# A layer norm's inverse root, in the attention layers, on POOL in place of DVE

## The chip, the cores and the metric

One Trainium2 chip, one of its cores. The time is the device time of one execution of the whole program in microseconds; lower is better. The engines are named as in the profile: PE (TensorE) multiplies matrices, DVE (VectorE), ACT (ScalarE) and POOL (GpSimd) work element by element, SP (SyncE) issues the transfers. Each engine takes its instructions in the order in which they were built, and an instruction whose operands aren't ready holds up all that stand behind it on its engine.

## The reference

A residual stream `x` of 2048 tokens by 640 runs through four layers. Layers 1 and 3 mix by a Fourier transform, layers 2 and 4 are attention over a window of 256 tokens, with 32 heads of 20.

```python
x = x + A(_layernorm(x))      # Real(DFT_seq(DFT_hidden(x))), as products with matrices
x = x + B(_layernorm(x))      # attention
x = x + A(_layernorm(x))
x = x + B(_layernorm(x))

def _layernorm(x, axis=-1, eps=1e-5):
    m = jnp.mean(x, axis=axis, keepdims=True)
    v = jnp.var(x, axis=axis, keepdims=True)
    return (x - m) / jnp.sqrt(v + eps)

def B(x):                      # q, k, v from x @ wqkv, H = 32, Dh = 20, W = 256
    scores = einsum("bhqd,bhkd->bhqk", q, k) * Dh ** -0.5
    scores = where(0 <= idx[:, None] - idx[None, :] < W, scores, -1e9)
    return einsum("bhqk,bhkd->bhqd", softmax(scores), v) -> (B, S, D) @ wo
```

## The kernel before

The tokens stand in 16 tiles of 128, a token to a partition. All products are made of pairs of 16-bit parts (a high part and a low part of what is left), so every operand is split: ACT writes the high part, DVE or POOL the low one. `spectral` computes the Fourier layers, `attention` the others; both are called twice, and this text counts attention layers 0 and 1.

**The loop of an attention layer** runs over `g`, 256 steps (16 tiles by 16 pairs of heads) and 12 more that finish. In each step `scores(g)` lets PE write the scores of one tile and pair into the tile `sp`, of which there is one buffer; DVE masks them (L1054) and takes their maximum `m` (L1058). Every fourth step the maxima are split into `tops` (L1064, L1065), and PE's transposes of them (`hand_on`, `copy_tops`) put them into `qs`. Seven steps later `by_key` makes the scores again, keys first, into `tp`, ACT turns them into weights `ptq` (L1102), and every other step POOL cuts the window's edges out of them with two selects (L1107, L1109). Thirteen steps later PE multiplies four heads' weights with `v` into `pv` (`values`); `back` divides, and POOL makes the two parts `os` of the output (L1153, L1154). What else PE has to do is handed out between these by a list of units `fill` (`run_fill`, `turn_unit`): the projections of the next block of two tiles (results `qf`, then `early`), products with `wo` (`out_tile`; for the last block `last_out`, in pieces), transposes.

**The norms in this loop** are generators in a queue `slow`; `slow_step`, once a step, runs the first of them up to its next `yield`. `rows_norm` normalises the two tiles of the block after next, `next_norm` (in layer 0 alone) each output tile for the Fourier layer that follows. Both use `norm_steps` and then `split` the result `lny` into `xs`: ACT the high part (L165), POOL the low one (L166); PE transposes `xs` later (`rows_turn`, `next_turn`), ACT and DVE copy the result (`xto`, `early`). For one tile a norm is two steps of statistics (L129, L132), two of the root (L138 to L142: eight instructions of one column, an estimate by bits and three rounds of Newton, each reading what the one before wrote) and the last step `lny` (L154). For the two tiles of `rows_norm` the statistics of both come first, then both roots, then both last steps. In `spectral` the norms are called with `act`, so that ACT makes the last step and DVE one instruction more (L146); that form is not touched.

**What sets the order.** The code is traced in the order in which the loop calls it, and a scheduler places each engine's instructions from that order and their dependencies. What `slow_step` traces stands under `tc.issue_after(topped[0])`: instructions of DVE are kept behind the newest maximum or part of the tops. This holds on DVE alone; instructions that the same step traces on another engine are not tied to it. In an attention layer PE's products and SP's transfers keep the traced order (`in_turn`).

After step 256 of layer 0 the last two tiles' products are finished in `last_out`, their norms are run by `next_norm` in the loop's last steps and in the loop behind it, eight at a time, and the next Fourier layer's first splits (`cc` from `cq` and `cs`, by `take_c`, on POOL, ACT and DVE) and products (`Hidden.stage`) stand among them.

Of the kernel before, what the change touches and what calls it, by code (L numbers as in the profile page):

```python
# [15 lines left out]
OP = mybir.AluOpType  # L16
# [46 lines left out]
def body(ctx: ExitStack, tc: tile.TileContext, x_in, cmat, whid, wqkv, wo, out):  # L63
    nc = tc.nc
# [42 lines left out]
    normed = [None]  # L107
# [14 lines left out]
    def norm_steps(xs, ys, act=False):  # L122

        n = len(xs)
        mv = keep.tile([P, n, 2], F32, tag=f"lnmv{n}", name="lnmv", bufs=2)
        for k, x in enumerate(xs):
            st = keep.tile([P, 2, 6], F32, tag="lnst", name="lnst", bufs=2)
            for h in range(2):
                nc.vector.bn_stats(st[:, h], x[:, h * 320:(h + 1) * 320])  # L129
                if h == 0:  # L130
                    yield
            nc.vector.bn_aggr(mv[:, k], st.rearrange("p a b -> p (a b)"))  # L132
            yield
        t = keep.tile([P, 3, n], F32, tag=f"lnt{n}", name="lnt", bufs=2)
        ts = nc.vector.tensor_scalar
        for k in range(n):
            h, g, u = (t[:, m, k:k + 1] for m in range(3))
            ts(h, mv[:, k, 1:2], 1e-5, -0.5 * X_UP ** -2, op0=OP.add, op1=OP.mult)  # L138
            ts(g.bitcast(I32), h.bitcast(I32), -0.5, ROOT, op0=OP.mult, op1=OP.add)
            for m in range(3):  # L140
                ts(u, g, g, h, op0=OP.mult, op1=OP.mult)  # L141
                normed[0] = ts(g, u, 1.5, g, op0=OP.add, op1=OP.mult).ins  # L142
                if m == 0:
                    yield
            if act:
                normed[0] = ts(u, mv[:, k, 0:1], g, -1.0, op0=OP.mult, op1=OP.mult).ins  # L146
            yield
        for k, x in enumerate(xs):
            g, u = t[:, 1, k:k + 1], t[:, 2, k:k + 1]
            y = keep.tile([P, D], F32, tag="lny", name="lny", bufs=2)  # L150
            if act:
                nc.scalar.activation(y, x, AF.Identity, bias=u, scale=g)
            else:
                normed[0] = ts(y, x, mv[:, k, 0:1], g, op0=OP.subtract, op1=OP.mult).ins  # L154
            ys.append(y)
            yield

    def layer_norm(xs):
        ys = []
        for _ in norm_steps(xs, ys, True):  # L160
            pass
        return ys
# [181 lines left out]
    def spectral(layer, res_src, hidden, first):  # L344
        with ExitStack() as st:
# [95 lines left out]
            def side_norm(s):  # L441
                x, ys = load_x(s), []
                for _ in range(3):
                    yield 1
                for _ in norm_steps([x], ys, True):
                    yield 1
                split_x(s, ys[0], nc.gpsimd)
                yield 1
# [853 lines left out]
```

## Time and profile before

| what | value |
| --- | --- |
| runs, median of 3 (lowest to highest) | 2277.91 us (2277.79 to 2279.62) |
| the profiled execution | 2273.16 us |
| its span, first to last instruction | 2271.4 us |
| granted clock of PE | 0.987 |
| busy, of the span: PE, DVE, POOL, ACT | 94%, 72%, 61%, 57% |
| attention layer 0, attention layer 1 | about 595 to 1210 us, 1700 to 2271 us |

The profile is one execution. Busy is the time in which an engine had at least one instruction under way; a matmul's record holds its way through the pipeline too, so PE's 94% overstates how much of its peak is used. The chain of waits is followed back from the last instruction: at each step to the instruction that released it, or to the one before it on the same engine; it tells which work was late, not by how much. A group's row holds line, engine, operation, names and shapes, count, busy time, mean of one in ns, and the idle time ahead of it. A row of waits holds the total in us, how often, and the longest. The trace names tiles by their role: `x` stands for the residual tiles.

### The profile page before, as it was taken

The page shows a single profiled execution, that of the slowest core. Times are in us where ns is not written, and L with a number is a line of the kernel's source. Part 1 is how long each engine was busy: PE and PEld are TensorE (multiplying, and loading weights), DVE is VectorE, ACT ScalarE, POOL GpSimd, SP SyncE. Part 2 cuts the span into 40 slices and gives each one's busy share as a digit, 9 for nine tenths or more (in the row PEclk, how much of TensorE's full clock was granted, in tenths as well). Part 3 has the DMA queues.
Part 4 walks back from the last instruction along what each step waited for, and adds up shares of the span by engine and source line. Part 5 has one row for each costly group of instructions (what it writes and reads, how often), then busy time and mean ns, then how long its engine had stood idle before and what let it go on. Part 6 is the DMA issues. An engine that isn't in the chain of part 4 may idle for free.

```text
span 2271.4 us, 55086 instructions
## 1 busy us (share of the span) xinstructions
PE 2132.5 (94%) x21985; PEld 1498.7 (66%) x21985; DVE 1632.5 (72%) x3577; ACT 1291.8 (57%) x2159; POOL 1387.0 (61%) x1788
## 2 busy tenths in 40 slices
PE   7989889899899999999898999999998999999997
PEld 4757666667666666677555777777676666777664
DVE  7886758866678787886756858585757777777664
ACT  6434455443367777777754443433434777777775
POOL 5775868857355665565445858586674545566443
PEclk9999999999999999999999999999999999999999
DMA  7664646454532322333324536363643323332231
GB/s 247 214 214 136 211 162 213 162 194 165 138 83 68 94 75 72 92 90 86 129 76 142 195 130 207 112 207 137 254 125 97 81 57 83 93 95 56 56 76 36
DMA packets 187605, 292.94 MB, mean 129 GB/s; under 512 B 13908, under 2 KB 120660, under 8 KB 178004
## 3 DMA queue, kind: packets, MB, share of 16 engines
q1 hardware_dynamic: 187348, 289.43, 40.9%
q8 instruction: 172, 2.82, 0.5%
q14 instruction: 85, 0.70, 0.1%
HBM read 202.51 MB, written 86.87 MB: 127 GB/s over the span
## 4 chain that ended last, share of the span: by engine, by line
PE 61%; DVE 14%; issue 5%; POOL 4%; ACT 3%; DMA 2%; SPq 0%; DVEq 0%; POOLq 0%; ACTq 0%
PE pf L116 25%; PE pv L116 8%; PE y L116 8%; PE z L116 5%; PE x L116 5%; PE sp L116 5%; DVE m L1058 3%; DVE sp L1054 3%; PE tp L116 3%; PE pt L116 2%; DVE cc L488 2%; ACT ptq L1102 1%; DMA x<-x2d 1%; DVE lnt L141 1%; PE acc L116 1%
## 5 line engine op out<-in xcount | busy, mean ns | idle before, releaser
L116 PEld LDWEIGHTS <-cc 128*128 128x128 f16 x5376 | 526.7, 98 | 220.6 <-issue 17.6
L1102 ACT ACTIVATE ptq<-tp,shift,alpha 128x768 f32<-128x768 f32 (+2 forms) x512 | 486.7, 951 | 176.1 <-PE tp L116 166.0
L116 PEld LDWEIGHTS <-big 128*128 128x128 f16 x4320 | 410.6, 99 | 148.7 <-issue 34.0
L1058 DVE TENSOR_REDUCE m<-sp 128x2 f32<-128x512 f32 (+1 forms) x512 | 344.9, 674 | 16.7
L1054 DVE COPY_PREDICATED sp<-mask,sp 128x256 f32<-128x256 int32 x448 | 191.0, 426 | 203.0 <-PE sp L116 186.7
L1107 POOL TENSOR_SCALAR_AFFINE_SELECT ptq<-ptq 128x512 f32<-128x512 f32 x224 | 145.4, 649 | 261.2 <-ACT ptq L1102 260.5
L116 PE MATMUL pf<-early,big 128*128 128x256 f16 x2400 | 304.5, 273 | 0.0
L485 ACT ACTIVATE cc<-cs 128x512 f16<-128x512 f32 x256 | 151.6, 623 | 241.3 <-POOL cs L478 119.2
L116 PE MATMUL y<-zc,cc 128*128 128x320 f16 x1728 | 266.3, 301 | 6.4 <-DVE pf L511 6.1
L488 DVE SCALAR_TENSOR_TENSOR cc<-cs,cc 128x512 f16<-128x512 f32 x256 | 252.2, 1000 | 13.2 <-ACT cc L485 12.9
L116 PE MATMUL pf<-big 128*128 128x320 f16 x1680 | 243.7, 304 | 17.2 <-DVE zc L256 8.3
L488 DVE SCALAR_TENSOR_TENSOR cc<-cq,cc 128x512 f16<-128x512 f32 x192 | 192.2, 1002 | 0.1
L1109 POOL TENSOR_SCALAR_AFFINE_SELECT ptq<-ptq 128x512 f32<-128x512 f32 x256 | 164.1, 641 | 43.7 <-ACT ptq L1102 43.7
L116 PE MATMUL pv<-ptq,v 128*32 128x128 f32 (+1 forms) x3840 | 183.8, 331 | 0.0
L116 PE MATMUL z<-zc,cc 128*128 128x320 f16 x1152 | 179.7, 301 | 3.7 <-DVE res L511 3.7
L116 PE MATMUL x<-zc,cc 128*128 128x320 f16 x1152 | 180.2, 301 | 0.0
L116 PE MATMUL sp<-ks,qs 62*128 62x256 f16 (+1 forms) x1792 | 154.3, 249 | 17.2 <-DVE m L1058 15.1
L1079 ACT ACTIVATE qs<-pt 2x512 f16<-2x512 f16 x224 | 131.4, 586 | 47.8 <-PE pt L116 45.2
L116 PE MATMUL pf<-big,early 128*128 128x320 f16 x960 | 157.6, 300 | 0.8 <-DVE x L879 0.8
L116 PE MATMUL tp<-qs,ks 62*128 62x128 f16 x2688 | 150.6, 217 | 4.4 <-ACT ptq L1102 3.4
L116 PE MATMUL pf<-bo,ot 128*128 128x320 f16 x840 | 141.9, 302 | 6.1 <-DVE ot L952 6.1
L116 PEld LDWEIGHTS <-ks 62*128 62x128 f16 x3008 | 116.5, 94 | 43.3 <-DVE m L1058 20.1
(143 smaller groups left out, 3495.6 us busy)
## 6 DMA issues: line engine op xcount, KB each, us to landing
cq<-in_cmat_dram SPq DMA_DIRECT2D x64, 1024.0 KB
accd<-res SPq DMA_DIRECT2D x96, 320.0 KB
res<-accd SPq DMA_DIRECT2D x96, 320.0 KB
x<-x2d SPq DMA_DIRECT2D x64, 320.0 KB
qkd<-early SPq DMA_DIRECT2D x160, 128.0 KB
ks<-qkd SPq DMA_DIRECT2D x108, 160.0 KB
qs<-qkd SPq DMA_DIRECT2D x84, 160.0 KB
x2d<-res SPq DMA_DIRECT2D x32, 320.0 KB
```

The costliest lines, as they stand in the source:

```text
L116: i = getattr(nc.tensor, what)(*args, **kw)
L141: ts(u, g, g, h, op0=OP.mult, op1=OP.mult)
L485: nc.scalar.activation(cc[m][:, 0], f, AF.Copy, scale=C_UP)
L488: nc.vector.scalar_tensor_tensor(cc[m][:, 1], f, C_UP, cc[m][:, 0], op0=OP.mult, op1=OP.subtract)
L1054: nc.vector.copy_predicated(sp[:, :, 2 * P:3 * P], mask[:, None, :].to_broadcast([P, 2, P]), far)
L1058: topped[0] = nc.vector.tensor_reduce(TOP[g // 4][:, g % 4], sp[:, :, c0:3 * P], axis=AX.X, op=OP.max).ins
L1079: nc.scalar.activation(o, handed[n][rs].rearrange("r (i p) t -> r i p t", i=2), AF.Copy)
L1102: nc.scalar.activation(q[:, h:h + 2, a0 + first:a0 + 3], tp[:, :, first * P:3 * P].rearrange("p a (b c) -> p a b c", c=P), AF.Sigmoid, bia ...
L1107: nc.gpsimd.affine_select(out=q[:, :, a0], in_=q[:, :, a0], pattern=[[0, 4], [-1, P]], base=0, channel_multiplier=1, compare_op=OP.is_gt, ...
L1109: ins = nc.gpsimd.affine_select(out=q[:, :, a0 + 2], in_=q[:, :, a0 + 2], pattern=[[0, 4], [1, P]], base=0, channel_multiplier=-1, compare ...
```

## The change

The eight instructions of the root are issued on POOL where a norm is called without `act`, that is in the attention layers, 40 columns in all (28 in layer 0: 12 of `rows_norm`, 16 of `next_norm`; 12 in layer 1). One `yield` more puts the last step one step of the loop later. The last step stays on DVE.

```diff
--- before.py
+++ after.py
@@ -132,7 +132,7 @@
             nc.vector.bn_aggr(mv[:, k], st.rearrange("p a b -> p (a b)"))
             yield
         t = keep.tile([P, 3, n], F32, tag=f"lnt{n}", name="lnt", bufs=2)
-        ts = nc.vector.tensor_scalar
+        ts = nc.vector.tensor_scalar if act else nc.gpsimd.tensor_scalar
         for k in range(n):
             h, g, u = (t[:, m, k:k + 1] for m in range(3))
             ts(h, mv[:, k, 1:2], 1e-5, -0.5 * X_UP ** -2, op0=OP.add, op1=OP.mult)
@@ -145,13 +145,15 @@
             if act:
                 normed[0] = ts(u, mv[:, k, 0:1], g, -1.0, op0=OP.mult, op1=OP.mult).ins
             yield
+        if not act:
+            yield
         for k, x in enumerate(xs):
             g, u = t[:, 1, k:k + 1], t[:, 2, k:k + 1]
             y = keep.tile([P, D], F32, tag="lny", name="lny", bufs=2)
             if act:
                 nc.scalar.activation(y, x, AF.Identity, bias=u, scale=g)
             else:
-                normed[0] = ts(y, x, mv[:, k, 0:1], g, op0=OP.subtract, op1=OP.mult).ins
+                normed[0] = nc.vector.tensor_scalar(y, x, mv[:, k, 0:1], g, op0=OP.subtract, op1=OP.mult).ins
             ys.append(y)
             yield
```

In the changed file all lines behind the added ones have numbers higher by two.

**In the middle of layer 0** the order changes like this. The first two pieces are DVE in the kernel before and in the changed one, at the norm of one output tile. (`lnmv` holds mean and variance, `lnt` the root, `o` and `r` belong to the division of the output, `pt` is a transpose.)

```order
L1065 SCALAR_TENSOR_TENSOR tops0_77<-m_8835,tops0_77 128x4x2 [waits DVE_49]
L138 TENSOR_SCALAR lnt_8962<-lnmv_8889 128x1
L139 TENSOR_SCALAR lnt_8962<-lnt_8962 128x1 [waits DVE_49]
L141 TENSOR_SCALAR lnt_8962<-lnt_8962 128x1 [waits DVE_49]
L142 TENSOR_SCALAR lnt_8962<-lnt_8962 128x1 [waits DVE_49]
L1054 COPY_PREDICATED sp_8990<-mask_73,sp_8990 128x2x128 [waits PE_49]
L1058 TENSOR_REDUCE m_8996<-sp_8990 128x2 [waits DVE_49]
L141 TENSOR_SCALAR lnt_8962<-lnt_8962 128x1
L952 COPY early_8399<-pt_9012 128x640 [waits PE_49]
```

```order
L1067 SCALAR_TENSOR_TENSOR tops0_77<-m_8835,tops0_77 128x4x2 [waits DVE_49]
L1056 COPY_PREDICATED sp_8990<-mask_73,sp_8990 128x2x128 [waits PE_49]
L1060 TENSOR_REDUCE m_8996<-sp_8990 128x2 [waits DVE_49]
L954 COPY early_8399<-pt_9012 128x640 [waits PE_49]
L1056 COPY_PREDICATED sp_9029<-mask_73,sp_9029 128x2x128 [waits DVE_49,PE_49]
L1060 TENSOR_REDUCE m_8996<-sp_9029 128x2 [waits DVE_49]
L1056 COPY_PREDICATED sp_9063<-mask_73,sp_9063 128x2x128 [waits DVE_49,PE_49]
L1060 TENSOR_REDUCE m_8996<-sp_9063 128x2 [waits DVE_49]
L156 TENSOR_SCALAR lny_9081<-x3_8498,lnmv_8889,lnt_8962 128x640 [waits Pool_49]
```

The root's instructions (behind the rows shown before come L142, L141 and L142 again) are gone from between the maxima. The last step L156, which stood behind the second maximum after the root's start, stands behind the third and waits for POOL. The same place on POOL in the changed kernel:

```order
L1109 AFFINE_SELECT ptq_8804<-ptq_8804 128x4x128 [waits Activation_49]
L1111 AFFINE_SELECT ptq_8804<-ptq_8804 128x4x128
L138 TENSOR_SCALAR lnt_8962<-lnmv_8889 128x1 [waits DVE_49]
L139 TENSOR_SCALAR lnt_8962<-lnt_8962 128x1 [waits Pool_49]
L141 TENSOR_SCALAR lnt_8962<-lnt_8962 128x1 [waits Pool_49]
L142 TENSOR_SCALAR lnt_8962<-lnt_8962 128x1 [waits Pool_49]
```

Two more pairs of L141 and L142 follow, then the parts of `os` and the next selects. All eight stand together, and each waits for the one ahead of it.

**At the end of layer 0**, where the scores are done, the norms of tiles 12 and 13 stood on DVE one through the other:

```order
L129 BN_STATS lnst_17074<-x3_16580 128x6 [waits DVE_49]
L141 TENSOR_SCALAR lnt_16948<-lnt_16948 128x1 [waits DVE_49]
L132 BN_AGGR lnmv_17073<-lnst_17074 128x2 [waits DVE_49]
L142 TENSOR_SCALAR lnt_16948<-lnt_16948 128x1 [waits DVE_49]
L138 TENSOR_SCALAR lnt_17137<-lnmv_17073 128x1 [waits DVE_49]
L154 TENSOR_SCALAR lny_17026<-x3_16311,lnmv_16882,lnt_16948 128x640 [waits DVE_49]
L139 TENSOR_SCALAR lnt_17137<-lnt_17137 128x1 [waits DVE_49]
```

Seven more steps of tile 13's root, its last step (which comes ahead of the copy `ot` that PE waits for) follow there. In the changed kernel tile 12's norm is done earlier, and tile 13's stands so:

```order
L129 BN_STATS lnst_16950<-x3_16617 128x6
L881 SCALAR_TENSOR_TENSOR x3_16617<-pf_16895,beta_72,x3_16617 128x320 [waits PE_49]
L129 BN_STATS lnst_16950<-x3_16617 128x6 [waits DVE_49]
L132 BN_AGGR lnmv_16949<-lnst_16950 128x2 [waits DVE_49]
L156 TENSOR_SCALAR lny_17107<-x3_16617,lnmv_16949,lnt_16997 128x640 [waits DVE_49,Pool_49]
L954 COPY ot_17004<-pt_17011 128x384 [waits PE_49]
L1152 RECIPROCAL r_17047<-pv_7322 128x8 [waits PE_49,Activation_49]
```

The last step comes right behind L132 and waits for POOL, and `ot` behind it. On POOL the root stands there like this, with two selects behind its first instruction:

```order
L1155 CAST os_16304<-o_16920 128x2x80 [waits DVE_49]
L1156 TENSOR_TENSOR os_16304<-o_16920,os_16304 128x2x80 [waits Pool_49]
L138 TENSOR_SCALAR lnt_16997<-lnmv_16949 128x1 [waits DVE_49]
L1109 AFFINE_SELECT ptq_16915<-ptq_16915 128x4x128 [waits Activation_49]
L1111 AFFINE_SELECT ptq_16915<-ptq_16915 128x4x128
L139 TENSOR_SCALAR lnt_16997<-lnt_16997 128x1 [waits Pool_49]
L141 TENSOR_SCALAR lnt_16997<-lnt_16997 128x1 [waits Pool_49]
L142 TENSOR_SCALAR lnt_16997<-lnt_16997 128x1 [waits Pool_49]
```

Two more pairs follow, then the low part of `xs`. On ACT, first before, then changed:

```order
L1102 ACTIVATE ptq_16880<-tp_16939,shift_75,alpha_71 128x2x384 [waits PE_49]
L1079 ACTIVATE qs_15466<-pt_16934 2x2x2x128
L165 ACTIVATE xs_17069<-lny_17026 128x640 [waits DVE_49]
L1135 ACTIVATE pvs_16969<-pv_7322 128x256 [waits PE_49]
L1102 ACTIVATE ptq_16880<-tp_16971,shift_75,alpha_71 128x2x384 [waits PE_49]
L954 ACTIVATE ot_16988<-pt_16990 128x384 [waits PE_49]
L165 ACTIVATE xs_17221<-lny_17216 128x640 [waits DVE_49]
```

```order
L1081 ACTIVATE qs_15466<-pt_16952 2x2x2x128
L1104 ACTIVATE ptq_16915<-tp_16957,shift_75,alpha_71 128x2x384 [waits PE_49]
L1137 ACTIVATE pvs_16984<-pv_7322 128x256 [waits DVE_49,PE_49]
L167 ACTIVATE xs_17145<-lny_17107 128x640 [waits DVE_49]
L1104 ACTIVATE ptq_16915<-tp_16986,shift_75,alpha_71 128x2x384 [waits PE_49]
L956 ACTIVATE ot_17004<-pt_17006 128x384 [waits PE_49]
```

Before, ACT's `xs` of tile 12 stood ahead of the last sigmoid of that group and of `ot`, and that of tile 13 behind them. Now tile 13's stands ahead of them.

**The last two tiles** of layer 0 on DVE, before and now:

```order
L129 BN_STATS lnst_17328<-x3_16986 128x6 [waits DVE_49] x2
L852 SCALAR_TENSOR_TENSOR x3_17194<-acc_17197,beta_72,x3_17194 128x320 [waits DMAHW7_49,DMAHW1_49,PE_49]
L852 SCALAR_TENSOR_TENSOR x3_17194<-acc_17197,beta_72,x3_17194 128x320
L132 BN_AGGR lnmv_17327<-lnst_17328 128x2 [waits DVE_49]
L129 BN_STATS lnst_17348<-x3_17194 128x6 [waits DVE_49]
L138 TENSOR_SCALAR lnt_17332<-lnmv_17327 128x1 [waits DVE_49]
L129 BN_STATS lnst_17348<-x3_17194 128x6
```

```order
L129 BN_STATS lnst_17331<-x3_17002 128x6 [waits DVE_49] x2
L132 BN_AGGR lnmv_17330<-lnst_17331 128x2 [waits DVE_49]
L954 COPY xto_17148<-pt_17350 128x640 [waits DMAHW2_49,PE_49]
L854 SCALAR_TENSOR_TENSOR x3_17215<-acc_17218,beta_72,x3_17215 128x320 [waits DMAHW1_49,PE_49]
L156 TENSOR_SCALAR lny_17344<-x3_17002,lnmv_17330,lnt_17335 128x640 [waits DVE_49,Pool_49]
L854 SCALAR_TENSOR_TENSOR x3_17215<-acc_17218,beta_72,x3_17215 128x320
L129 BN_STATS lnst_17363<-x3_17215 128x6 [waits DVE_49] x2
L258 SCALAR_TENSOR_TENSOR zc_17419<-pf_17420,zc_17419 128x320 [waits DMAHW5_49,DMAHW4_49,Activation_49]
L132 BN_AGGR lnmv_17362<-lnst_17363 128x2 [waits DVE_49]
```

Before, both tiles' residual halves and statistics came first, then their roots one through the other. Now tile 14's last step, which waits for POOL, stands between the two residual halves (L854) of tile 15. On POOL root 14, the low part of `xs` 14 and root 15 follow each other there.

## The prediction

> **What bounds the kernel now.** I read the page first, then its slices as windows over the two attention layers, then the chain of waits, then who waited for whom.
>
> ```profile
> span 2271.4 us, 55086 instructions
> PE 2132.5 (94%) x21985; PEld 1498.7 (66%) x21985; DVE 1632.5 (72%) x3577; ACT 1291.8 (57%) x2159; POOL 1387.0 (61%) x1788
> 595.00:1165.00 570.00, 536.53 (x7042) 370.78 (x7040) 446.39 (x1157) 412.88 (x624) 311.65 (x563) 0.99 0.32 89
> 1700.00:2200.00 500.00, 483.19 (x6324) 336.43 (x6326) 362.28 (x896) 352.24 (x535) 267.86 (x508) 1.00 0.32 80
> ```
>
> The two window rows are attention layer 0 (595 to 1165 us, ahead of its last products) and layer 1 (1700 to 2200 us); their columns after the length are PE, PEld, DVE, ACT and POOL. PE is busy 536.5 of 570 and 483.2 of 500 us, DVE 446.4 and 362.3, POOL 311.7 and 267.9. So PE is the bound nearly everywhere, DVE is second, and POOL is idle 45% of the time.
>
> ```profile
> by line: PE pf L116 29.1%; PE pv L116 14.7%; PE sp L116 9.2%; issue 6.9%; DVE sp L1054 6.3%; DVE m L1058 6.1%; PE tp L116 4.9%; PE pt L116 4.6%; ACT ptq L1102 1.9%; DVE lnt L141 1.8%; DVE lnt L142 1.3%; DVE o L1151 1.2%; DVE r L1150 0.9%; D
> by line: PE pf L116 34.4%; PE pv L116 16.3%; PE sp L116 10.4%; PE tp L116 5.7%; DVE m L1058 5.1%; DVE sp L1054 4.4%; PE pt L116 3.7%; issue 3.5%; ACT ptq L1102 2.5%; PE acc L116 1.4%; PE y L116 1.2%; DMA x<-x2d 1.1%; PE z L116 0.9%; DVE top
> ```
>
> These are the chain's shares in layer 0 and in layer 1 (1700 to 2272 us). In layer 0 the lines L141 and L142, two of the root's four, carry 1.8 + 1.3 = 3.1% of 570 us = 17.7 us. In layer 1 no line of the root is among the named ones, the smallest of which has 0.9% of 572 us.
>
> ```profile
> PEld L116 <- DVE m L1058: 23.2, 51, 1.3
> PE sp L116 <- DVE m L1058: 12.1, 20, 1.1
> PE pt L116 <- DVE xto L952: 5.4, 8, 1.2
> PEld L116 <- DVE ot L952: 5.1, 7, 1.1
> PE pf L116 <- DVE ot L952: 2.7, 5, 0.8
> ...
> PEld L116 <- DVE m L1058: 30.4, 73, 1.2
> PE sp L116 <- DVE m L1058: 11.7, 23, 1.0
> ```
>
> The first five rows are layer 0, the last two layer 1. The time in which the matmuls themselves stood is small: 12.1 + 5.4 + 2.7 = 20.2 us in the rows shown of layer 0, 11.7 in layer 1. The weight loads' 23.2 + 5.1 and 30.4 us lie partly beside a matmul that still runs. Why DVE can hold PE at all, a piece of the chain of layer 0 shows:
>
> ```profile
> 741.17 0.07 DVE lnt L138
> ...
> 741.98 0.44 DVE sp L1054
> ```
>
> The score tile sp is single, so PE's next scores wait for L1058's maximum, and the maximum waits for L1054; between the end of one maximum, where L138 starts (741.17 us), and the next L1054 (741.98) stand 0.81 us of root on DVE.
>
> **The change part by part.** What leaves DVE is 40 columns of eight steps, 28 in layer 0 and 12 in layer 1 (x84 and x36 of L141, three to a column):
>
> ```profile
> L141 DVE TENSOR_SCALAR lnt<-lnt 128x1 f32<-128x1 f32 x84 | 22.6, 269 | 1.9
> L142 DVE TENSOR_SCALAR lnt<-lnt 128x1 f32<-128x1 f32 x84 | 17.7, 212 | 2.1
> L139 DVE TENSOR_SCALAR lnt<-lnt 128x1 int32<-128x1 int32 x28 | 4.2, 150 | 0.7
> L138 DVE TENSOR_SCALAR lnt<-lnmv 128x1 f32<-128x1 f32 x28 | 4.0, 144 | 0.0
> ...
> L141 DVE TENSOR_SCALAR lnt<-lnt 128x1 f32<-128x1 f32 x36 | 9.7, 270 | 0.8
> ```
>
> In layer 0 that is 22.6 + 17.7 + 4.2 + 4.0 = 48.5 us, in layer 1 12/28 of it, 20.8; together 69.3 us, and some 20 ns of gap a step besides. The statistics ahead (L129, L132) and the last step (L154) stay on DVE.
>
> What of this is on PE's path? The chain bounds layer 0 from above: 17.7 us, and for L138 and L139 in proportion to their busy time (8.2 to 40.3) another 3.6, 21 us. From below it is 0: DVE's time on the chain and PE's work are so nearly equal that PE may just do its fill products there. In between: the chain holds DVE for 17.6% (its lines in the row shown) and issue for 6.9% of 570 us, 140 us, while PE stood 20 to 48 us for DVE by the rows above, 0.14 to 0.35 of it; times 21 us this gives 3 to 7. A stretch with a root in it is longer than the others, so its last part is what PE waits for, and I take 8 us for layer 0. Layer 1, with 12 columns and a PE that waits as much for DVE: 8 x 12/28 = 3. Gain 11 us, bounds 0 and 21 + 9.
>
> POOL gets 320 instructions of one column. The trace of before has none like them; the nearest rows:
>
> ```profile
> L1109 POOL TENSOR_SCALAR_AFFINE_SELECT ptq<-ptq 128x512 f32<-128x512 f32 x256 | 164.1, 641 | 43.7 <-ACT ptq L1102 43.7
> L335 POOL CAST early<-qf 128x256 f16<-128x256 f32 x160 | 66.5, 416 | 50.0 <-ACT qf L334 49.7
> L1154 POOL TENSOR_TENSOR os<-o,os 128x160 f16<-128x160 f32 x128 | 63.7, 497 | 9.8
> L1153 POOL CAST os<-o 128x160 f16<-128x160 f32 x128 | 41.2, 322 | 104.9 <-DVE o L1151 103.4 <-DVE lnt L139 1.5
> L89 POOL MEMSET shift<- 128x1 f32 x1 | 0.1, 99 | 0.0
> ```
>
> A copy takes 322 ns for 160 and 416 for 256 elements, so about 0.165 us for none; the select's 641 ns for 512 fits that slope (0.98 ns an element) with 0.14. A fill of one column takes 99 ns. Idle ahead of L1154, which reads what L1153 just wrote, is 9.8 us / 128 = 77 ns: each step of the root waits so for the one before. DVE pays 60 ns for a scalar from memory (150, 212, 269 ns for none, one, two); with as much on POOL the eight steps take 2 x 0.17 + 3 x (0.29 + 0.23) = 1.9 us, with waits 2.5 us a column. Bounds: 1.4 us (all at 99 ns, with waits) and 5.1 us (each like L1154 with its wait, 0.57, and 60 ns for each of nine scalars). I take 2.5, nearest to the copies' start. 40 columns are 100 us in POOL's 490 us of idle time in the two windows, so POOL does not become the bound. What is queued behind the root on POOL are the selects of ptq, which PE's pv products wait for:
>
> ```profile
> 750.91 0.64 POOL L1107 TENSOR_SCALAR_AFFINE_SELECT ptq<-ptq 128x512 f32<-128x512 f32 x1 [0.93 <-ACT ptq L1102]
> 751.50 0.64 POOL L1109 TENSOR_SCALAR_AFFINE_SELECT ptq<-ptq 128x512 f32<-128x512 f32 x1
> ...
> 755.78 1.51 PE L116 MATMUL pv<-ptq,v 128*32 128x256 f32 x32
> ```
>
> The group's last select ends at 752.14 us, its products start at 755.78: 3.6 us of room, and 0.93 us that POOL stood before the pair. A root of 2.5 us ahead of it fits. So inside the layers I cost POOL's work at nothing; its cover is these 4.5 us.
>
> The other new wait is DVE's last step on POOL. Inside the layers POOL may begin as soon as L132 is done, and the last step stands four slots of the loop later (570 us for the layer's 256 slots: 2.2 us each), so 2.5 us is hidden. At the end of layer 0 it isn't: no scores are left there, and the order puts L132 and the last step one right behind the other. There tile 13's norm stands so on the chain of before:
>
> ```profile
> 1157.98 0.12 DVE lnmv L132
> 1158.29 0.60 DVE lny L154
> 1158.91 0.74 ACT xs L165
> 1160.06 0.88 ACT ptq L1102
> 1160.94 0.39 ACT ot L954
> 1161.37 0.34 PE pt L116 x3
> ```
>
> L132 ends at 1158.10 and the first of two last steps follows at once, because its root was done while DVE waited for other things. ACT then does xs, pvs, the sigmoid and ot, and PE goes on at 1161.37. In the changed order DVE and ACT have a single last step there, tile 13's, whose root POOL does after L132 and with two selects (1.3 us) behind its first step. L132 comes earlier, at about 1157.5 (tile 12's root is no longer in its way), then 2.5 + 1.3 + some 0.1 to each engine: last step 1161.4 to 1162.0, xs to 1162.8, sigmoid to 1163.8, ot to 1164.2, so PE goes on 2.8 us later. Loss 2.8 us (1.7 to 5.4 at the bounds of the root).
>
> Tiles 14 and 15 end the layer:
>
> ```profile
> 1192.01 1.01 DVE L852 SCALAR_TENSOR_TENSOR x<-acc,beta,x 128x320 f32<-128x320 f32 x2
> 1192.93 0.20 DVE L132 BATCH_NORM_AGGREGATE lnmv<-lnst 128x2 f32<-128x12 f32 x1
> ...
> 1202.76 1.35 PE pf L116 x5
> ```
>
> Before, tile 14's L132 comes behind both residual halves (L852) of tile 15, both roots run side by side on DVE among the next layer's splits, and PE goes on at 1202.76. Now L132 comes ahead of these halves, at about 1192.0, and tile 15's second half stands on DVE behind tile 14's last step. POOL does root 14, the low part of xs 14 and root 15, one after the other. I add from 1192.2: 2.5 of root, 0.6 of last step, then, as POOL's 1.4 us of xs behind ACT's 0.74 ends at about 1197.8 and DVE's half, statistics and L132 (0.5 + 0.9 + 0.7 with a split) at 1197.5, another 2.5, 0.6, 0.74 and six handovers of 0.1: PE goes on near 1202.1. I take 0.7 us of gain (2 of gain to 4.5 of loss).
>
> The added yield puts every later step of a norm one slot back. Transposes, loads into the freed x tiles and stores move on PE and SP with it (order changes only in layer 0 on those two). The rows are needed half a block of 32 slots later, so I cost it at 0, plus or minus 4 us for the new order of layer 0.
>
> Last, POOL's and DVE's nearness:
>
> ```profile
> L1064 DVE TENSOR_SCALAR tops<-m x128: 170/182/1390, 607.3 to 2241.7; 128x8 f16<-128x8 f32 x128
> L1064 DVE TENSOR_SCALAR tops<-m 128x8 f16<-128x8 f32 x128 | 35.7, 279 | 0.2
> L1065 DVE SCALAR_TENSOR_TENSOR tops<-m,tops 128x8 f16<-128x8 f32 x128 | 29.9, 234 | 0.7
> ```
>
> L1064 takes 170 ns at best and 279 in the mean, L1065, as small, 234: 128 x (109 + 64) = 22 us of DVE's time. If these delays grow with POOL's busy time, 100 us on 580, they add 4 us on DVE and, at 0.35, 1 us to the span.
>
> The Trainium skill (Perfetto Trace Analysis, Optimizing Scalar/DVE Operations) warns that moving work between these two engines might not help, since they share a read port that one of them holds exclusively. The longest L1064, 1390 ns, agrees. By that rule the 11 us would be nothing, and the sum -0 + 2.8 - 0.7 + 1 = +3 us instead of -8.
>
> Sum: -11 + 2.8 - 0.7 + 1 = -8 us. The profiled execution took 2273.16 us, its span 2271.4; the runs' median is 2277.91, 4.8 us above it, and I lay the sum on the median: **2270 us**. A measurement of this kernel can tell about 0.2%, 4.6 us, from no change.
>
> **The rivals.** First, hidden: PE has other products to do wherever DVE got shorter. For it: 94% busy PE, and the matmuls' own waits for DVE's maximum of only 12 us a layer. Gain 3 instead of 11: 2278, within 0.2%.
>
> Second, slower: POOL's steps are dear. If a step with its wait takes 0.56 us or more, the root passes the 4.5 us of cover and PE's pv products wait for selects. At the bound of 5.1 us the lateness is 0.6 us for each root that stands ahead of a group's last select, say half of 40, 12 us; the end of layer 0 loses 5.4 + 4.5, 2277.9 - 11 + 12 + 10 = 2289. For it: POOL has no row with scalars from memory. Against: every POOL row shown starts at 0.1 to 0.19 us.
>
> Third, the port: POOL's 77 us of added busy time each hold DVE off for as long as they last, and DVE wins nothing: 2277.9 - 0 + 2.8 - 0.7 + 1 = 2281, no change. Against: L1064's median is 182 ns, so most of them are held by nothing though POOL is busy for over half of the time.
>
> Fourth, that the chain is the true measure: 21 + 9 us gone, 2250.
>
> **How the numbers follow.** The forecast's case, 5 to 18 us faster, 0.50; the chain's whole, 0.05; hidden, 0.19; port 0.06; dear steps 0.13; a worse order in layer 0, past the 4 us allowed for, 0.07. Faster 0.55, same 0.25, slower 0.20. The range leaves out the fourth rival and most of the second: 2256 to 2284; the forecast's own is 2260 to 2273.
>
> **What would show it.** L138 to L142 on POOL, x320, near 0.2 to 0.3 us, some 80 ns idle ahead of each; DVE 69 us less busy, its root gone from the chain in layer 0; PE's waits for DVE's maximum in layer 0 down from 35 to some 27 us. Near 1160 us a wait of DVE for POOL's root, and PE standing 2 to 3 us longer. A POOL step over 0.5 us, late selects, or DVE waiting for POOL inside the layers would make it wrong.

## The result and the profile after: slower

The changed kernel took 2285.17 us (median of 11 runs, 2281.68 to 2289.81). The kernel before, run beside it, took 2271.65 us (11 runs, 2269.24 to 2279.62). The ratio is 1.0051, with a 95% interval of 1.0040 to 1.0062: 0.5%, some 12 us, slower, where 8 us faster was forecast. The median of 2277.91 us on which the forecast was laid is that of the three slowest of these eleven runs of before; laid on 2271.65 it would have been 2264. The profiled execution has a span of 2284.5 us.

The page, then the two windows over the attention layers, as they were shown of before (busy time of PE, PEld, DVE, ACT, POOL in each):

```profile
span 2284.5 us, 55127 instructions
...
PE 2134.9 (93%) x21985; PEld 1499.4 (66%) x21985; DVE 1580.0 (69%) x3257; ACT 1292.8 (57%) x2159; POOL 1478.4 (65%) x2108
...
595.00:1165.00 570.00, 528.08 (x6949) 364.93 (x6948) 405.19 (x938) 407.84 (x616) 361.98 (x756) 0.99 0.31 87
1700.00:2200.00 500.00, 479.69 (x6245) 334.29 (x6244) 343.41 (x791) 346.17 (x528) 297.83 (x599) 1.00 0.32 81
```

What was to move has moved. POOL has 320 instructions more and 91 us more of busy time. DVE has 52.5 us less; the root's records were 69.3 us in sum, but they overlap those of their neighbours. And yet in the 570 us of layer 0 PE does 6949 matmuls where it did 7042.

The price of the steps on POOL, and three forms of DVE that would show it being held off, the two small ones (L1066, L1067) and the last step (groups by shape: busy time, mean ns of one, idle time ahead):

```profile
L1066 DVE TENSOR_SCALAR tops<-m 128x8 f16<-128x8 f32 x128 | 35.2, 275 | 0.2
...
L156 DVE TENSOR_SCALAR lny<-x,lnmv,lnt 128x640 f32<-128x640 f32 x40 | 31.0, 775 | 9.0 <-POOL lnt L142 9.0
...
L1067 DVE SCALAR_TENSOR_TENSOR tops<-m,tops 128x8 f16<-128x8 f32 x128 | 28.2, 220 | 0.7
...
L141 POOL TENSOR_SCALAR lnt<-lnt 128x1 f32<-128x1 f32 x120 | 42.2, 351 | 11.9
L142 POOL TENSOR_SCALAR lnt<-lnt 128x1 f32<-128x1 f32 x120 | 32.5, 271 | 12.3
L138 POOL TENSOR_SCALAR lnt<-lnmv 128x1 f32<-128x1 f32 x40 | 8.3, 208 | 12.9 <-DVE lnmv L132 9.9
L139 POOL TENSOR_SCALAR lnt<-lnt 128x1 int32<-128x1 int32 x40 | 8.2, 206 | 3.5
```

A column takes 0.21 + 0.21 + 3 x (0.35 + 0.27) = 2.3 us and some 0.6 of gaps, 2.9 us (2.5 was estimated). The small steps that were L1064 and L1065 take 275 and 220 ns in the mean, before 279 and 234, and the last step 775, before 862 (its row is shown further down): the root's steps on POOL do not hold DVE off. The 9.0 us of DVE's wait for the root are three waits, all at the end of layer 0 (below).

The chain of waits of layer 0 and PE's longest waits there (total, times, longest us); the last piece is two rows of before that the prediction doesn't show:

```profile
by line: PE pf L116 28.3%; PE pv L116 13.8%; PE sp L116 8.9%; issue 5.7%; PE tp L116 4.8%; PE pt L116 4.2%; DVE sp L1056 3.7%; DVE m L1060 3.4%; POOL early L338 2.4%; ACT ptq L1104 2.1%; POOL ptq L1111 1.5%; POOL lnt L141 1.5%; DMA res<-acc
```

```profile
PE sp L116 <- DVE m L1060: 14.6, 22, 1.7
PE pt L116 <- DVE xto L954: 6.7, 8, 2.2
PE tp L116 <- ACT ptq L1104: 6.4, 8, 1.4
PE pf L116 <- DVE ot L954: 4.5, 4, 1.4
PE pt L116 <- ACT early L956: 3.9, 7, 0.8
```

```profile
PE tp L116 <- ACT ptq L1102: 2.1, 7, 0.5
...
PE pt L116 <- ACT early L954: 0.5, 2, 0.3
```

DVE's L141 and L142 are gone from the chain and DVE's mask and maximum have 7.1% of it, before 12.4%. In their place stand POOL's low part of `early` (L338) with 2.4% and one line of POOL's root (L141) with 1.5%. PE waits 14.6 us for the maximum, before 12.1; 6.4 us for ACT's sigmoid, the `ptq` row, before 2.1; 3.9 us for `early` out of `pt` on ACT, before 0.5.

**Where in the program.** Between the starts of the first and the 241st maximum of layer 0, the same work in both kernels, lie 515.8 us before and 527.9 after. From the first to the last maximum of layer 1 it is 522.9 and 524.0. So the loss is in layer 0. The table splits it: for each pair of successive PE instructions of the same kinds, the distance of their starts less the shortest eighth's, summed by what released the second.

| us, first to 241st maximum of layer 0 | all | sp from DVE's maximum | tp from ACT's sigmoid | pt from DVE's xto | pt from ACT's early |
| --- | --- | --- | --- | --- | --- |
| before | 515.8 | 11.4 | 5.2 | 5.2 | 0.4 |
| changed | 527.9 | 14.3 | 8.4 | 7.6 | 5.0 |
| slot alone (e1) | 529.9 | 15.2 | 2.9 | 10.1 | 5.0 |
| POOL alone (e2) | 519.4 | 11.7 | 8.8 | 5.9 | 0.4 |
| two steps on DVE (e3) | 509.4 | 9.7 | 4.5 | 4.4 | 0.4 |
| POOL does it too (e10) | 519.0 | 12.7 | 8.3 | 6.0 | 0.4 |
| the same, four qf (e15) | 517.6 | 13.1 | 5.0 | 7.0 | 0.1 |
| two steps, POOL too (e14) | 516.9 | 10.8 | 8.8 | 5.2 | 0.4 |
| copy first (e13) | 522.9 | 14.8 | 8.6 | 3.8 | 5.0 |

These are single executions, and some are far from the median of their kernel: e2's took 2286.1 us (median 2275.5), e10's 2284.0 (2277.7), e15's 2282.3 (2275.5). In each of them PE's granted clock is also 0.50 for some us at a time, at different work: of the stretch in the table 10 us lie at that clock in the kernel before (1107 to 1117 us) as in the changed one (1119 to 1125 us, for example), 17 in e1, 14 in e2, some 7 in e10, e14 and e15, and 3 to 4 in e3 and e13. So differences of a few us in the first column say little. The verdicts below go by the ratios of all runs.

### The profile page after: what moved, and what is told of

Read it like the earlier page. It is cut to its first block, busy times and chain, and to the rows that moved or that the text cites. A ratio compares the mean times of both kernels' runs of the same rounds, so it can differ in the third digit from the quotient of the medians.

```text
span 2284.5 us, 55127 instructions
## 1 busy us (share of the span) xinstructions
PE 2134.9 (93%) x21985; PEld 1499.4 (66%) x21985; DVE 1580.0 (69%) x3257; ACT 1292.8 (57%) x2159; POOL 1478.4 (65%) x2108
## 4 chain that ended last, share of the span: by engine, by line
PE 60%; DVE 9%; POOL 7%; DMA 5%; issue 4%; ACT 3%; SPq 1%; DVEq 0%; POOLq 0%; ACTq 0%
PE pf L116 24%; PE pv L116 8%; PE y L116 8%; PE x L116 5%; PE z L116 5%; PE sp L116 5%; PE tp L116 3%; PE pt L116 2%; DVE m L1060 2%; DVE sp L1056 2%; DVE cc L490 2%; ACT ptq L1104 1%; DMA x2d<-res 1%; DMA ks<-qkd 1%; DMA res<-accd 1%
```

## The experiments

The change has two parts, and the order on PE follows the extra yield alone: with the root on POOL and no extra yield PE's rows are those of before but for 20, with the yield and the root on DVE those of the changed kernel but for 28. So the parts can be run one by one.

**The extra slot alone (e1).**

```diff
             yield
+        if not act:
+            yield
         for k, x in enumerate(xs):
```

> The root stays on DVE; only the extra yield is kept, so PE has nearly the changed kernel's order in attention layer 0. Theory A (the slot's new order in layer 0 is what costs): +10 to +16 us against before, all of it in attention layer 0, and layer 1 unmoved; as DVE still has its root, rather at the upper end. Theory B (POOL's steps cost: late selects, late low parts, or the port shared with DVE): 0 to +3 us.

Ratio 1.0033 (1.0018 to 1.0048), some 8 us, so the slot costs by itself: less than the 10 to 16 of theory A, more than the 3 of theory B.

**POOL alone (e2).** The changed kernel without these two lines.

> The root is on POOL without the extra yield, so PE keeps the order of before, but for one piece of 10 rows. Theory A (the slot's order costs): no loss, 0 to -8 us against before, as DVE is 69 us less busy. Theory B (POOL's steps cost): +10 to +14 us, as for the whole change, or more, since the last step now waits for POOL a slot earlier.

Ratio 1.0010 (0.9995 to 1.0025), +2 us: theory B's 10 us are out, and of theory A only its bound, no gain, lies within the interval. DVE has 69 us less of root here, and no gain shows.

**Two steps of eight (e3).**

```diff
             for m in range(3):
-                ts(u, g, g, h, op0=OP.mult, op1=OP.mult)
-                normed[0] = ts(g, u, 1.5, g, op0=OP.add, op1=OP.mult).ins
+                if act:
+                    ts(u, g, g, h, op0=OP.mult, op1=OP.mult)
+                    normed[0] = ts(g, u, 1.5, g, op0=OP.add, op1=OP.mult).ins
```

> The six Newton steps of the root are left out in the attention layers, so the norm's scale there is the first guess only; the two steps that are left stay on DVE, nothing goes to POOL, and PE keeps the order of before, but for 10 rows. It takes 40 x 6 instructions, 58 us, from DVE. Theory C (DVE's root was on PE's path, as forecast): 0.83 x 11 = 9 us faster. Theory D (hidden: PE does its fill products in that time anyway): within 3 us of before.

Ratio 0.9939 (0.9923 to 0.9954), 14 us faster. DVE's root was on PE's path, and by more than forecast. So e2 must pay for something: 14 us of gain are gone.

**The slot in next_norm only (e4).** The root on POOL, the extra yield behind a flag that only next_norm sets.

> The root is on POOL in all attention norms, but the extra yield only in next_norm, which runs in attention layer 0 alone; rows_norm has the slots of before. Theory A: the delay of the output tiles' norms, 16 of layer 0's 28 columns, gives about half or more of the loss, +6 to +12 us. Theory B: the same as the whole change, +12 us, since POOL's work is the same.

Ratio 1.0037 (1.0025 to 1.0050), some 6 us above e2 and 3 below the changed kernel (4 either way): the output tiles' norms seem to carry the larger part of the slot's cost.

**What POOL's root pushes back.** In the changed kernel's timeline (start, length, engine; in brackets the idle time ahead and what ended it) this is one of the places where it hurts:

```profile
992.05 0.19 POOL L138 TENSOR_SCALAR lnt<-lnmv 128x1 f32<-128x1 f32 x1
...
994.70 0.27 POOL L142 TENSOR_SCALAR lnt<-lnt 128x1 f32<-128x1 f32 x1
994.91 0.64 POOL L1109 TENSOR_SCALAR_AFFINE_SELECT ptq<-ptq 128x512 f32<-128x512 f32 x1
995.50 0.65 POOL L1111 TENSOR_SCALAR_AFFINE_SELECT ptq<-ptq 128x512 f32<-128x512 f32 x1
996.08 0.40 POOL L337 CAST early<-qf 128x256 f16<-128x256 f32 x1
996.57 0.67 POOL L338 TENSOR_TENSOR early<-qf,early 128x256 f16<-128x256 f32 x1
...
997.28 0.39 ACT L336 ACTIVATE qf<-pf 128x256 f32<-128x256 f32 x1 [2.03 <-POOL early L338]
...
998.75 0.99 ACT L1104 ACTIVATE ptq<-tp,shift,alpha 128x768 f32<-128x768 f32 x1
...
999.80 0.34 PE L116 MATMUL tp<-qs,ks 62*128 62x128 f16 x6 [1.37 <-ACT ptq L1104]
```

ACT writes `qf` from a product, POOL makes `early` of it, and there are two `qf`. With a root of 2.9 us and two selects ahead of the casts, the older `qf` is free only at 997.24. ACT stands 2.03 us, its sigmoid comes late, and PE's scores by key wait 1.37 us for it. In the changed kernel's layer 0 ACT waits so 4 times, in the kernel before not once:

```profile
ACT qf L336 <- POOL early L338: 7.6, 4, 2.2
```

The next four runs have no extra yield. Four buffers `qf` in the attention layers (in their own pool, `bufs=4`):

> As the root on POOL without the extra yield (which was 2 us slower than before, where 58 us less of root on DVE alone had been 14 us faster), but with four buffers qf in the attention layers in place of two, so that ACT can write the next one while POOL's casts of the last ones stand behind a root. Theory Q (ACT stands for POOL's late casts, its sigmoid comes late, and PE waits for that): 4 to 8 us faster than with two buffers, so -2 to -6 us against before, and ACT's waits for early (5.1 us in layer 0, 3.5 in layer 1) gone. Theory T (the loss is at the end of layer 0, where the root is in nobody's shadow): as with two buffers, +2 us.

Ratio 0.9993 (0.9979 to 1.0007), 4 us better than e2 by the ratios, with 5 us either way; what backs it is the trace, in which ACT's wait for `qf` behind `early` falls from 5.1 us (e2) to 0.3 in layer 0, and e15 below, where the same step is worth 4 us again.

> The kernel before with four buffers qf in place of two and nothing else: what the buffers are worth by themselves. Theory Q and theory T both: 0 to -2 us, since ACT waited for qf before only 3.8 us, all in layer 1.

Ratio 0.9994 (0.9984 to 1.0005): the buffers by themselves are worth nothing that shows.

The other place is the end of layer 0:

```diff
-                yield from norm_steps([x3], ys)
+                yield from norm_steps([x3], ys, pool=i < NT - 3)
```

> As the root on POOL without the extra yield, but the roots of tiles 13, 14 and 15, the last three norms of layer 0, stay on DVE. Theory T: 4 to 8 us faster than with these on POOL, so -2 to -6 us against before, as PE no longer waits near 1170 and 1208 us. Theory Q: 2 to 3 us faster than with these on POOL, 0 to -1 us against before.

Ratio 1.0007 (0.9992 to 1.0022), not to be told from e2: 0.7 us better, with 5 us either way. So theory T's 8 us are out, its 4 are not. With four `qf` the same step (e8 against e5) gives 3 us, with 4 either way.

> Both: the last three roots on DVE, the others on POOL, no extra yield, four buffers qf. If Q and T are all that POOL costs, it comes near what the shorter DVE alone was worth: -8 to -14 us against before. If POOL's steps cost in a third way (late selects, late low parts, a shared port), it stays within 4 us of before.

Ratio 0.9980 (0.9967 to 0.9993), 4 us faster than before, but not the 8 to 14 us that DVE's relief is worth. Q and T are not all that POOL costs.

**POOL works for nobody (e10).** The kernel before; POOL does the eight steps a second time into a tile of its own:

```diff
+            if not act:
+                h2, g2, u2 = (t2[:, m, k:k + 1] for m in range(3))
+                tp2 = nc.gpsimd.tensor_scalar
+                tp2(h2, mv[:, k, 1:2], 1e-5, -0.5 * X_UP ** -2, op0=OP.add, op1=OP.mult)
...
```

> The kernel before, in its own order, with its root on DVE; POOL runs the same eight steps a column as well, into a tile that nothing reads. So POOL's queue has the root's 2.7 us a column in it, but nobody waits for its result and DVE wins nothing. Theory P (POOL's casts and selects standing behind the root are what POOL's root costs, with ACT's wait for qf the largest): +6 to +10 us against before, with ACT waiting some 5 us for early in layer 0. Theory L (it costs because the last step waits longer for the root): within 2 us of before.

Ratio 1.0019 (1.0008 to 1.0029), +4 us. ACT's waits come back although nobody reads the result:

```profile
ACT qf L343 <- POOL early L345: 4.9, 3, 2.0
```

So the queue costs, but theory P's 6 to 10 us were too many for a DVE that still has its root. With four `qf`:

> As the run in which POOL does the root's steps for nobody (+4 us against before), but with four buffers qf. Theory Q (the queue's price is ACT's wait for qf behind POOL's casts): 0 to +1 us against before, PE's waits for the sigmoid back from 8.3 to about 5 us. If the price lies in selects, low parts or a shared port: still +3 to +4 us.

Ratio 1.0002 (0.9990 to 1.0014). The waits for the sigmoid are back at 5.0 us, and the cost is within the noise: where DVE still has its root, most of the queue's price is the wait for `qf`.

**Both: two steps on DVE, POOL busy for nobody (e14).**

> DVE does only two of the eight steps (the Newton steps are left out in the attention layers, so the scale there is the first guess), and POOL does all eight steps as well, into a tile that nothing reads. So DVE is as free as with the root on POOL, POOL's queue is as full, but no last step waits for POOL. Theory L (what the root on POOL costs beyond POOL's queue is the wait of the last step for POOL's result): the two effects add, -13 + 4 = -9 us against before (-6 to -11). Theory N (DVE's gain is lost as soon as POOL is busy, whoever waits): near what the root on POOL gives, 0 to +3 us.

Ratio 0.9989 (0.9976 to 1.0001). It lies between the theories, nearer to N: of 14 us of gain 11 are gone (with 5 either way), with no last step waiting for POOL. In the table, e14 takes 7.5 us more than e3, and 4.3 of it are waits for the sigmoid (8.8 for 4.5). It may be that with a short DVE queue PE arrives earlier at the next limit, so that ACT's lateness counts in full; no run shows that. A shared port it is not: from e3 to e14 POOL's busy time grows from 1388.3 to 1475.6 us, and DVE's falls from 1586.1 to 1579.6. e2, where the last step does wait for POOL, lies 0.0021 above e14, some 5 us, just about what the two intervals can tell. Its trace shows where DVE stood for the root, at the end of layer 0 and nowhere else:

```profile
DVE lny L154 <- POOL lnt L142: 9.3, 4, 3.0
```

In none of the traces with the root on POOL does DVE wait for it, by 0.15 us or more, before the layer's last maximum.

**The root earlier on POOL (e16).** In e8 each column's root is traced right behind its own statistics (its yields stay where they were):

```diff
             nc.vector.bn_aggr(mv[:, k], st.rearrange("p a b -> p (a b)"))
+            if pool:
+                for _ in root(k):
+                    pass
             yield
```

> As the version with the last three roots on DVE, four buffers qf and no extra yield (-4 us), but POOL's root is traced right behind the statistics of its own column, two to four slots ahead of the last step and one root at a time; the number of yields and PE's order are those of before. Theory L (the last step waits for POOL): 2 to 6 us faster than without it, -6 to -10 us against before. Theory N: as without it, -4 us.

Ratio 0.9980 (0.9969 to 0.9991), as e8: theory L fails here too, as it must when no last step inside the layers waits.

**The slot: what stands ahead of a copy.** Another place, one of four of its kind in the changed kernel's layer 0:

```profile
1004.79 0.45 PE L116 MATMUL pt<-idh,xs 128*128 128x128 f16 x5
...
1005.32 0.69 DVE L1060 TENSOR_REDUCE m<-sp 128x2 f32<-128x512 f32 x1
1005.93 0.81 DVE L156 TENSOR_SCALAR lny<-x,lnmv,lnt 128x640 f32<-128x640 f32 x1
1006.66 0.48 DVE L954 COPY xto<-pt 128x640 f16<-128x640 f16 x1
...
1007.19 0.38 PE L116 MATMUL pt<-idh,tops 128*66 128x128 f16 x4 [1.13 <-DVE xto L954]
```

The transposes are done at 1005.24, but the copy that empties `pt`, of which there is one bank, stands on DVE behind the last step of another norm, 0.81 us. The transposes of `tops` wait 1.13 us, and all of PE behind them. One slot earlier, in the kernel before, that last step comes in a slot without such a copy. Counted in DVE's order (program text, no times), a copy out of `pt` has a last step right ahead of it, or one row further, 7 times in the changed kernel and 3 times before.

The first try to move them: the norm's step is traced behind the slot's transposes in every fourth slot.

> The changed kernel, with PE's order untouched, but in every fourth slot, the one in which the loop issues the transposes of a norm's rows, the norm's step is traced behind these transposes and not ahead of them, so that on DVE the copy that frees the only bank pt comes ahead of a last step of 0.67 us. Up to the 241st maximum of layer 0 the changed kernel takes 12.1 us more than before, with PE waiting 7.6 us for xto copies (before 5.2) and 14.3 us for DVE's maxima (11.4). Theory S (the extra slot moves last steps ahead of these copies): 4 to 6 us faster than the changed kernel, so +6 to +8 us against before, and the waits for xto back near 5 us. Theory O (the new order on PE itself costs, two transposes right behind each other through one bank): within 2 us of the changed kernel, +10 to +13 us.

Ratio 1.0055 (1.0041 to 1.0069), as the changed kernel. It looked like theory O, but DVE's order shows that all 7 last steps were still ahead of their copies: a copy depends on transposes that PE does later, and the scheduler put the step first all the same. This run tells nothing on S. Two more were run with the same edit, with the last three roots on DVE and four `qf`:

> As the version with the last three roots on DVE, four buffers qf and no extra yield (4 us faster than before), with the norm's step behind the transposes in every fourth slot. PE's order is that of before. Theory S: 0 to 3 us more, -4 to -7 us against before, since without the extra yield few last steps stand in that slot. Theory O: as without it, -4 us.

> The same with the extra yield put back, so that PE has the changed kernel's order: all that differs from the run before it is the slot. Theory S: within 3 us of the version without the slot, -2 to -6 us against before. Theory O: 5 to 9 us slower than without the slot, +1 to +4 us against before.

0.9987 (0.9977 to 0.9998) without and 1.0002 (0.9992 to 1.0012) with the slot. As 6 of the places remain in the second, the slot's 0.0015 there is no verdict on O either.

The second try holds the step behind the copy: the copy is what the next steps are issued after.

```diff
                 if k:
-                    nc.vector.tensor_copy(o[:, k, d0:d1], ptv[:, d0:d1])
+                    topped[0] = nc.vector.tensor_copy(o[:, k, d0:d1], ptv[:, d0:d1]).ins
...
                 if m == 3 or m == 0 and credit[0] + ns > TURN_ROOM or g >= NG + HAND_LAG:
                     turn_unit()
+                slow_step()
```

> The changed kernel with PE's order untouched; every norm's step is traced behind the transposes of its slot and kept on DVE behind their copy. In the changed kernel's order 7 copies out of pt stand on DVE with a last step right ahead of them or one row further, in the kernel before 3; the run that traced the step behind in every fourth slot left all 7 there, here 2 are left. Theory S (these last steps hold the one bank pt): waits for xto from 7.6 to about 4 us up to the 241st maximum of layer 0, 3 to 6 us faster than the changed kernel, +6 to +9 us against before. Theory O (PE's own order): within 2 us of the changed kernel, +10 to +13 us.

Ratio 1.0021 (1.0008 to 1.0033): of the changed kernel's 0.0051, 0.0030 is gone, 7 us (4 either way), with PE's order untouched. At the same place the copy now goes first, and PE's waits in layer 0 show it:

```profile
1002.84 0.69 DVE L1060 TENSOR_REDUCE m<-sp 128x2 f32<-128x512 f32 x1
1003.44 0.48 DVE L954 COPY xto<-pt 128x640 f16<-128x640 f16 x1
1003.84 1.77 DVE L156 TENSOR_SCALAR lny<-x,lnmv,lnt 128x640 f32<-128x640 f32 x1
...
1003.98 0.33 PE L116 MATMUL pt<-idh,tops 128*66 128x128 f16 x3 [0.41 <-DVE xto L954]
```

```profile
PE pt L116 <- ACT early L956: 3.9, 7, 0.8
PE pt L116 <- DVE xto L954: 3.3, 8, 0.9
```

The waits for `xto` fall from 6.7 to 3.3 us. As PE's order is the same in both, the two traces can be laid side by side: e13 gains 3.7 us at four such places (1.6 and three times 0.7). It gains 3 more at another one, at the end of layer 0, where `ot`, also a copy out of `pt`, now goes ahead of the last step of tile 13 that waits for POOL's root; PE's wait for it, first in the changed kernel and then in e13:

```profile
1175.24 0.48 PE L116 MATMUL pt<-idh,os 128*128 128x128 f16 x3 [4.33 <-ACT ot L956]
```

```profile
1166.06 0.33 PE L116 MATMUL pt<-idh,os 128*128 128x128 f16 x3 [1.19 <-ACT ot L956]
```

(Another 3 us between the two traces are granted clock, 0.50 from 1119 to 1125 us in the changed kernel and 1.00 at the same work in e13.) So theory S holds, and it is some 4 of the slot's 9 us. The 3.9 us of PE's waits for `early` on ACT stay, as they must if they come from PE's own order (three transposes in a slot that had two). Nor do last steps ahead of copies explain e4: it has 3 such places, as many as before, and its waits for `xto` in layer 0 are no longer than in e2, yet it lies 6 us above e2. So theory O, PE's own order, is not settled and may well be the other half.

**Everything taken out, with the slot (e17) and without (e18).**

> The changed kernel, extra yield and all, with everything that was found to cost taken out: the norm's steps behind the copies out of pt (2 of the 7 were left by that alone, here 1), the last three roots on DVE, four buffers qf. The same with steps behind in every fourth slot only, which left 6 of these places, took as long as before (+0.4 us). Theory S with Q and T: 3 to 5 us faster than that, -3 to -5 us against before, as the version without the extra yield. If PE's own order costs too: +0 to +2 us.

Ratio 0.9983 (0.9970 to 0.9996), 4 us faster than before, as e8 without the slot. But e8 has not had its copies put first; the next run has.

> The early root on POOL (last three on DVE, four qf, no extra yield: -5.8 us against before) with the norms' steps behind the copies out of pt; 1 such place is left of 3, but PE's order changes by 5% of its rows as well. By theory S 0 to 2 us better than without it, -6 to -8 us; if any new order of PE costs some us, -2 to -4 us.

Ratio 0.9953 (0.9937 to 0.9970): some 10 us faster than the kernel before, the best version, and better than either theory had it. It is 7 us faster than e17 (5 either way), which has the slot, and 6 faster than e16, which has not had the copies put first. As the early root by itself changed nothing (e16 against e8), the slot still seems to cost where the copies go first. Its page and waits in layer 0:

```profile
span 2259.8 us, 55113 instructions
...
PE 2127.9 (94%) x21985; PEld 1496.4 (66%) x21985; DVE 1580.6 (70%) x3281; ACT 1289.4 (57%) x2159; POOL 1466.8 (65%) x2084
```

```profile
PE sp L116 <- DVE m L1072: 12.4, 20, 1.8
PE pt L116 <- DVE xto L966: 4.9, 9, 1.0
...
PE tp L116 <- ACT ptq L1116: 2.2, 6, 0.7
```

DVE is as short as in the changed kernel (1580.6 us), and the three waits are within 0.3 us of those of before, or under them. Its order on PE differs from that of before in 530 of 36 387 rows, fewer than the expectation says; what this adds was not taken apart.

## Why the prediction was wrong

By ratios of runs, in us of 2273.7: the shorter DVE queue -14 (e3), POOL's queue +11 (e14 less e3), the last step's wait for POOL at the end of layer 0 +5 (e2 less e14), the slot +9 (changed less e2); sum +11. The sum closes by construction, as each term starts where the one before it ends, so it proves nothing by itself. The first term has 3 to 4 us to either side, each of the others 4 to 5, and another order of the steps would divide the sum otherwise: with the root on DVE the queue costs 4 (e10) and not 11. (In e3 and e14 DVE also keeps 11 us of the root.)

- **DVE's relief, -11 us.** The sign was right, the size rather small: 14 us for 58 of the 69 us of root. The forecast of PE's waits for the maximum (35 down to 27 us) failed: in the changed kernel they rose to 39 (14.6 of the matmuls, 24.8 of the weight loads), and even in e3 they are 32, so they did not measure the gain.
- **POOL's work inside the layers, 0.** This is the first step that failed. The price of the steps was near (2.9 for 2.5 us), and the cover that was named held: PE's products waited 1.2 us for a select in all. But of what is queued on POOL behind a root the prediction followed the selects alone. The casts of `qf` stand there too, ACT's next `qf` waits for them, and behind that on ACT stands the sigmoid. In place of 0 the runs show +11 us with the short DVE queue and +4 with the long one; four buffers `qf` take 4 us away in either case. What makes up the rest of the 11 is open.
- **The added yield, 0 plus or minus 4.** The second step that failed: +9 us. The prediction asked whether the rows are needed later, and not what the moved last step lands ahead of: some 4 us are lost at four places where it holds up the copy out of `pt` (e13). The rest comes with the yield too (e4), but no run shows by what; PE's own new order is the rival that is left.
- **The end of layer 0, +2.8 us.** It came as forecast, as far as a single trace tells. Tile 13 on the chain of waits:

```profile
1168.00 0.22 DVE lnmv L132
...
1168.30 0.19 POOL lnt L138
...
1168.57 0.64 POOL ptq L1109
1169.20 0.60 POOL ptq L1111
...
1172.25 0.28 POOL lnt L142
1172.55 0.62 DVE lny L156
...
1175.24 0.48 PE pt L116 x3
```

From L132 to PE it is 7.2 us, before 3.4. But L132 comes 0.8 us earlier, counted from the transposes of `tops` that PE does ahead of it (1167.05 and, before, 1156.15); from these to PE's next start it is 8.2 us, before 5.2, so 3.0 us are lost. In e13, where `ot` goes first, it is 5.1. Behind tiles 14 and 15 the first transposes wait 4.5 us, before 5.1 (0.7 of gain forecast). The runs' ratios don't resolve these (e7).
- **Contention, +1, and the port.** The root's short steps hold nothing: 275 for 279 ns. A long instruction does, as it did before the change. First the last step's row in the kernel before, then the longest one of e2, beside POOL's low part of another norm:

```profile
L154 DVE TENSOR_SCALAR lny<-x,lnmv,lnt 128x640 f32<-128x640 f32 x40 | 34.5, 862 | 0.1
```

```profile
998.05 1.78 DVE L154 TENSOR_SCALAR lny<-x,lnmv,lnt 128x640 f32<-128x640 f32 x1
998.07 1.40 POOL L166 TENSOR_TENSOR xs<-lny,xs 128x640 f16<-128x640 f32 x1
```

In the kernel before 7 of the 40 last steps take 1.4 to 1.6 us (median 0.67), and each ends 0.35 us after a low part on POOL that began 0.1 to 0.3 us ahead of it; in the changed kernel it is 3, and the last steps take 3.5 us less in sum. So this is no cost of the change. With the Trainium skill's rule (Perfetto Trace Analysis, Optimizing Scalar/DVE Operations) that the two engines share a read port which one of them holds exclusively, these traces agree for the long instructions and not for the root.
- **The rivals.** "Hidden" is refuted by e3, and "the chain is the true measure", 30 us, is twice what e3 shows. "Dear steps" needed 0.56 us a step and got 0.36. "The port" is refuted by e14, in which DVE is no busier beside the root on POOL. The slower outcome came from a worse order past 4 us, which had 0.07, and from a POOL queue that costs without dear steps, which no rival named.

Left open: some 7 of the 11 us of POOL's queue that four buffers `qf` don't give back, and some 5 of the 9 us of the slot that are not at the copies, PE's own new order or something else.

## What to carry to other kernels

When work is moved to an engine with idle time, follow every instruction that will stand behind it there, to who waits for its buffers; "idle 45%" and one cover with room do not say that the others have any. When a step is put a slot later, look at what it lands ahead of on its own engine, first at copies that empty a single buffer. And run the two halves of a change apart: here the queue on POOL and the wait at the layer's end ate a gain of 14 us, and the slot made a loss of 9.

## What was not expected of the hardware

An instruction of one column on POOL takes 0.19 us with immediate scalars, 0.27 with one scalar from memory and 0.34 with two (shortest 190, 265 and 342 ns), against 93 to 275 ns on DVE; with the gap of some 80 ns to the next dependent one the root takes 2.9 us there. A last step on DVE, of 0.67 us in the median, takes until 0.35 us after the end of POOL's low part of another norm (1.40 us) when the two start within some 0.3 us of each other, 1.4 to 1.8 us in all: seven times in the kernel before, three times in the changed one.
